# Attention and mixture of experts on one core: inputs laid out on the host, q as pairs of heads' dims by tokens

## The chip, the cores and the metric

The kernel runs on one core of one Trainium2 chip. The metric is the device time of one execution in microseconds (us), the median over runs. In the text PE is TensorE, DVE is VectorE, ACT is ScalarE, POOL is GpSimd, and SP is SyncE, which only issues DMAs here. A "batch" is one of the eight entries of the first axis of q, k and v.

## The reference, cut to what matters

All arrays are float32; q, k, v are 8 batches x 8 heads x 576 tokens x 64 dims. There is no softmax in the attention: k'v is a 64 x 64 matrix per head, and q times it is the output, which is then normalised over the 64 dims. The 4,608 token rows (512 wide) go to the one of 8 experts with the largest gate logit, through relu(x w1) w2 (512 -> 1024 -> 512), and are scaled by the gate's probability.

```
kv = np.einsum('bhsd,bhse->bhde', k, v)
out = np.einsum('bhsd,bhde->bhse', q, kv)
rms = np.sqrt(np.mean(out * out, axis=-1, keepdims=True) + 1e-06)
attn = out / rms * g_norm
x = attn.transpose(0, 2, 1, 3).reshape(B * S, H * D)
expert_idx = np.argmax(x @ w_gate, axis=1)
...
h = np.maximum(np.einsum('ecd,edf->ecf', disp, w1), 0.0)
y = np.einsum('ecf,efd->ecd', h, w2)
```

## The kernel before

The work has two stages. The first runs the attention batch by batch, routes each token, and, towards its end, already prepares the weights of one expert (the busiest after three batches) and runs that expert's first 384 rows. The second stage gathers the rows of the experts from a DRAM copy of x and runs the remaining products with weights split in two float16 halves.

Per batch the first stage does this:

- `load(b)` issues from SP, for each of k, v, q and each half of the heads (four heads), two DMAs into one of nine buffers (`NIO`): the odd partitions get four tokens per head (L708), the even partitions five (L709). The runs in DRAM are 1,024 and 1,280 bytes. A partition holds its tokens' rows, [head, token, dim].
- `kv_products` (L730) multiplies k' with v per head on PE, 80 small float32 products per batch. ACT or DVE copies the result to SBUF (`kvs`), PE transposes it (L754) and multiplies it with the gate's weights (L763). Then k'v and its gate columns (72 columns per head, `XW`) are copied into `kv_bd`. This tile is block-diagonal over two *tokens* of one head, so every block is written twice: eight copies per batch (L694 on ACT, L696 on DVE).
- `unit` transposes q on PE, two tokens x 64 dims at a time (L796, 20 transposes of 128 x 128 per batch), copies the result out of PSUM into `qt` (six copies per batch, L694 or L696), and multiplies `qt` with `kv_bd` (L814, 20 float32 products with 144 columns per batch; the trace shows each as two instructions). The result `op` is copied into the output tile `o_sb`, in ten pieces of which two are split in two, because the two tokens of that block belong to different heads.
- `squares` squares `o_sb` (ACT or POOL) and sums over the dims (L845 on DVE). `route` normalises, finds the expert and the position of every token with some 25 small operations, nearly all on DVE, and POOL writes the batch's rows to DRAM (L1023, L1021).

Every operation is given to a planner (`Plan`) with a cost per engine, dependencies, buffers (rings) and a key. The planner places the operations on a model of the engines, chooses between ACT, DVE and POOL where both can do one, and the resulting order is written out as each engine's program order. The second stage is placed by a second plan that starts from the engine times at which the first ended. The weights of the early expert are loaded in quarters between the last input loads (`WAFTER` counts the input loads that are issued before each quarter) and split by L358 (largest value), L387 (high half) and L393 (low half).

Of the kernel before, what the change touches and what calls it, by code (L numbers as in the profile page):

```python
# [12 lines left out]
F32 = mybir.dt.float32  # L13
# [15 lines left out]
NO = 3  # L29
NIO = 9  # L30
HALVED = (1,)
# [4 lines left out]
WAIT = {}  # L36
ISSUE = 1.6
AHEAD = 8.0
# [21 lines left out]
LOW = 36.5  # L60
LOAD = 1.66
WKEYS = ((29.5, 0.3), (38.0, 0.3))
# [13 lines left out]
class Ring:  # L76
# [84 lines left out]
def attention_moe_kernel(  # L161
# [12 lines left out]
    nc = tc.nc  # L174
    NB, H, S, D = q.shape
    N, DM = out.shape
    E = w_gate.shape[1]
# [9 lines left out]
    NT = NB * C  # L187
    W = E * NHI

# [9 lines left out]
    io = actx.enter_context(tc.tile_pool(name="io", bufs=1))  # L199
    ios = {}  # L200
    for i in range(NIO):
        flat = io.tile([P, HH * C * D], F32, name=f"in_sb{i}")
        t = flat.rearrange("p (h c d) -> p h c d", h=HH, c=C)
        (nc.vector if i % 3 == 1 else nc.gpsimd).memset(t[:, :, 0], 0.0)
        ios[i] = t, flat

# [75 lines left out]
    for i in range(2):  # L282
        kv_bds.append(cst.tile([P, H, 2, XW], F32, name=f"kv_bd{i}"))
    wgs = cst.tile([P, 2, 2, 2, E], F32, name="wgs")
# [369 lines left out]
    def slots(pool, reg_ap, s0=0):  # L654
# [3 lines left out]
        for tab_, nm in ((gidx_tab, "gi"), (sidx_tab, "si")):  # L658
# [9 lines left out]
    ps = {n: actx.enter_context(tc.tile_pool(name=f"ps_{n}", bufs=m, space=bass.MemoryType.PSUM))  # L668
          for n, m in (("a", 1), ("qp", 2), ("op", 2), ("x", 1), ("tab", 1), ("misc", 1))}
    bank = lambda n: ps[n].tile([P, 512], F32, tag=n, name=n)  # L670
# [10 lines left out]
    for i in range(NO):  # L681
# [4 lines left out]
    op = plan.op  # L686
    rings = {n: Ring(m) for n, m in (("in", NIO), ("a", 1), ("qp", 2), ("op", 2), ("x", 1),
                                     ("qt", 3), ("sq", 2), ("kvs", 1), ("kvt", 1), ("kv", 2), ("o", NO), ("lt", 1), ("ohh", 1),
                                     ("rhs", 1), ("ohl", 1), ("ss", NO), ("xg", 3), ("xm", 2), ("ysb", 2))}
# [10 lines left out]
    def load(b):  # L700
        ts = {}
        for j, (nm, half) in enumerate(ORDER):
            h = new("in")
            h.t, h.flat = ios[(len(rings["in"].holds) - 1) % NIO]

            def go(e, h=h, src={"k": k, "v": v, "q": q}[nm], hs=slice(half * HH, (half + 1) * HH)):
                rows = src[b, hs].rearrange("h (p n) d -> p h n d", n=2 * C - 1)
                nc.sync.dma_start(h.t[1:P:2, :, 1:C], rows[:, :, C:])  # L708
                nc.sync.dma_start(h.t[0:P:2], rows[:, :, 0:C])  # L709

            o = op(("S", ISSUE), go, [], (b - 2) * C + j * 0.8, takes=(h,))
            ts[nm, half] = h, op(("D", LOAD), None, [o], takes=(), uses=(h,))
            issued.append(o)
        return ts

    def kv_products(b, ts):
# [7 lines left out]
        def product(i):  # L724
            def go(e):
                a.t = a.t or bank("a")
                for c in range(C):
                    for g in range(2):
                        h = 2 * (i % 2) + g
                        nc.tensor.matmul(a.t[rows[g], i * D:(i + 1) * D], lhsT=kh.t[:, h, c, :], rhs=vh.t[:, h, c, :],  # L730
                                         start=(c == 0), stop=(c == C - 1))
# [12 lines left out]

        def spread(g, f):

            return op([("A", 0.42), ("V", 0.31)],
                      lambda e: copy(e, kv2[rows[f]].rearrange("p (i g) f x -> p i g f x", g=2)[:, :, g, f, 0:D],
                                     ks.t[rows[g]].rearrange("p (i x) -> p i x", i=HH)), done[0:1], key + 1.5, (kv,), (ks,))

# [17 lines left out]
        o = op(("T", 0.4), gates, [o], key + 1, (a3,), (kt,))  # L768
        done = [spread(g, f) for g in range(2) for f in range(2)]
        for g in range(2):  # L770
            for f in range(2):
                done.append(op([("A", 0.19), ("V", 0.13)],
                               lambda e, g=g, f=f: copy(
                                   e, kv2[rows[f]].rearrange("p (i g) f x -> p i g f x", g=2)[:, :, g, f, D:XW],
                                   a3.t[rows[g], 0:H * E].rearrange("p (i g x) -> p i g x", g=2, x=E)[:, :, g]),
                               [o] + done[4:], key + 2, (kv,), (a3,)))
        return kv, done


    UNITS = [(0, 0), (1, 0), (0, 1), (1, 1), (0, 2), (1, 2)]  # L780

    BLOCKS = ((0, 2), (1, 3), (4,))

    def unit(b, n, ts, kv, ready, oh):
        key = b * C + n * C / len(UNITS)
        o_sb, kv2 = oh.t, kv.t.rearrange("p h f x -> p (h f) x")
        qp, qt = new("qp"), new("qt")
        half, u = UNITS[n]
        qh, qd = ts["q", half]
        m = 2 * len(BLOCKS[u]) * P  # L790

        def turn(e):
            qp.t = bank("qp")
            for w, t in enumerate(BLOCKS[u]):
                for p in range(2):
                    nc.tensor.transpose(qp.t[:, (2 * w + p) * P:(2 * w + p + 1) * P],  # L796
                                        qh.flat[:, (t + C * p) * P:(t + C * p + 1) * P], ident)

        def keep(e):
            qt.t = at.tile([P, 512], F32, name="qt", bufs=3)  # L800
            copy(e, qt.t[:, 0:m], qp.t[:, 0:m])
# [4 lines left out]
        for w, t in enumerate(BLOCKS[u]):  # L806
            ph = new("op")

            def product(e, w=w, t=t, ph=ph):
                ph.t = bank("op")  # L810
                for p in range(2):
                    f = 2 * (half * HH + 2 * p + (t > 2))
                    x = kv2[:, f:f + 4:3] if t == 2 else kv2[:, f:f + 2]
                    nc.tensor.matmul(ph.t[:, p * 2 * XW:(p + 1) * 2 * XW], lhsT=qt.t[:, (2 * w + p) * P:(2 * w + p + 1) * P],  # L814
                                     rhs=x, start=True, stop=True)

            o = op(("T", 0.55), product, [kept] + ready, key, (ph,), (qt, kv))
            for s0, s1 in ((0, 1), (1, 2)) if t == 2 else ((0, 2),):

                def out_(e, t=t, ph=ph, s0=s0, s1=s1):  # L820
                    m0 = 2 * t + s0
                    h0, c0 = half * HH + m0 // C, m0 % C
                    copy(e, o_sb[:, c0:c0 + s1 - s0, h0:h0 + 3:2].rearrange("p c h x -> p h c x"),
                         ph.t[:, 0:4 * XW].rearrange("p (h c x) -> p h c x", h=2, c=2)[:, :, s0:s1])

                a = op([("A", 0.29), ("V", 0.37)] if s1 - s0 == 2 else [("A", 0.2), ("V", 0.22)], out_, [o], key, (oh,), (ph,))
                done += [((2 * t + i) % C, a) for i in range(s0, s1)]
        return done

    def squares(b, n, done, oh, ssh):  # L830

        key = b * C + (n + 1) * 0.8
        o_sb, ss = oh.t, ssh.t
# [453 lines left out]
    for b in range(NB):  # L1287
        oh, ssh = new("o"), new("ss")
        oh.t, ssh.t = o_sbs[b % NO], sss[b % NO]
        if b + 1 < NB:  # L1290
            tiles[b + 1] = load(b + 1)
        outs, sums = [], []
        for n in range(len(UNITS)):
            done = unit(b, n, tiles[b], *kvs[b], oh)
            outs += done
            if UNITS[n][0]:
                sums += [squares(b, c, [a for i, a in outs if i == c], oh, ssh) for c in ((0,), (1, 2), (3, 4))[UNITS[n][1]]]
            if n == 1 and b + 1 < NB:
                kvs[b + 1] = kv_products(b + 1, tiles[b + 1])
        route(b, oh, ssh, [a for _, a in outs], sums)  # L1300
        if b == PICK_AFTER:
            early_weights()
        if b == EARLY_AFTER:
            early_slots()
# [360 lines left out]


# [25 lines left out]
```

## Time and profile before

| | us |
|---|---|
| median of 3 runs (lowest, highest) | 553.29 (552.86, 553.55) |
| the profiled execution, its time | 553.62 |
| the profiled execution, its span from first to last instruction | 551.8 |
| PE busy | 520.2 (94% of the span) |
| DVE busy | 388.7 (70%) |
| ACT busy | 256.3 (46%) |
| POOL busy | 183.8 (33%) |

The busy shares are means over stages that look quite different, so the rows below are cut by stage. A busy engine in a row of the trace is not always an engine at its peak: consecutive matmuls overlap. The DMA share counts the time of packets on 16 DMA engines and can pass 1 where packets overlap.

### The profile page before, as it was taken

To read this page: it belongs to the slowest core of one execution; us is meant where nothing else is said; L and a number is where in the kernel's file an instruction comes from. 1 tells how busy PE (TensorE), PEld (TensorE's weight loads), DVE (VectorE), ACT (ScalarE), POOL (GpSimd) and SP (SyncE) were. 2 spreads that over 40 slices of the span, in tenths; PEclk is the share of its full clock that TensorE was granted. 3 is DMA by queue.
4 is the path that set the end of the run, shared out by engine and by line. 5 is a ranking of instruction groups with operands and counts; after the bars stand their busy time and mean duration, and the time that the engine had idled before them with its cause. 6 is when DMAs were issued, how large, how long until landed. Compare 5 with 4: busy or idle time off the path is not lost.

```text
span 551.8 us, 11752 instructions
## 1 busy us (share of the span) xinstructions
PE 520.2 (94%) x4458; PEld 358.2 (65%) x4458; DVE 388.7 (70%) x1042; ACT 256.3 (46%) x514; POOL 183.8 (33%) x187
## 2 busy tenths in 40 slices
PE   4999899877999999999999999999999999999995
PEld 4988888764546566457744764776487468648752
DVE  4388889999769899998998898387567526104800
ACT  1678677778224832745615633435162544211210
POOL 3011020624151462364427424442653264111011
PEclk9999999899999999999999999999999999999999
DMA  8999999952276869695677846464656153010000
GB/s 273 379 318 360 382 397 402 339 164 98 98 263 237 171 211 263 152 325 123 178 250 205 239 121 211 123 172 118 207 154 167 40 105 42 6 57 23 2 38 32
DMA packets 81903, 102.70 MB, mean 186 GB/s; under 512 B 39148, under 2 KB 63724, under 8 KB 80818
## 3 DMA queue, kind: packets, MB, share of 16 engines
q1 hardware_dynamic: 74240, 70.50, 43.1%
q0 software_dynamic: 7584, 31.38, 16.4%
q8 instruction: 37, 0.61, 0.4%
q14 instruction: 24, 0.20, 0.1%
q10 hardware_dynamic: 18, 0.02, 0.0%
HBM read 73.20 MB, written 20.68 MB: 170 GB/s over the span
## 4 chain that ended last, share of the span: by engine, by line
PE 33%; issue 27%; POOL 11%; DVE 9%; DMA 1%; POOLq 0%; ACT 0%; DVEq 0%
PE hp L548 15%; PE yp L595 14%; POOL out_dram L625 4%; POOL pair L481 3%; POOL xm L452 3%; PE op L548 2%; POOL xg L444 1%; DVE am L358 1%; DVE w1l L393 1%; DVE ss L845 1%; PE yp L604 1%; DMA raw<-in_moe_w_dram 1%; PE op L595 1%; DVE hl L556 1%; PE xp L463 0%
## 5 line engine op out<-in xcount | busy, mean ns | idle before, releaser
L548 PE MATMUL hp<-xs,w1h 128*128 128x320 f16 (+6 forms) x960 | 133.7, 292 | 2.4 <-DVE hl L556 1.1
L548 PEld LDWEIGHTS <-w1h 128*128 128x128 f16 x1024 | 99.4, 98 | 38.5 <-issue 3.3
L625 POOL DMA_INDIRECT out_dram<-ysb,si x42 | 43.9, 1046 | 156.2 <-ACT ysb L620 149.1
L595 PEld LDWEIGHTS <-hh 128*128 128x128 f16 x560 | 54.4, 98 | 62.8 <-issue 0.3
L553 ACT ACTIVATE hh<-hp 128x320 f16<-128x320 f32 (+7 forms) x64 | 40.9, 638 | 107.5 <-PE hp L548 98.0
L358 DVE TENSOR_REDUCE am<-raw 128x1 f32<-128x512 f32 x120 | 75.7, 674 | 4.1 <-DMA raw<-in_moe_w_dram 4.0
L548 PE MATMUL hp<-xs,w1l 128*128 128x320 f16 (+6 forms) x480 | 72.0, 292 | 0.0
L620 ACT ACTIVATE ysb<-yp,ysc 128x512 f32<-128x512 f32 (+5 forms) x41 | 28.1, 685 | 92.1 <-PE yp L595 85.7
L556 DVE SCALAR_TENSOR_TENSOR hl<-hp,hh 128x320 f16<-128x320 f32 (+7 forms) x64 | 47.5, 742 | 28.8 <-ACT hh L553 26.5
L595 PE MATMUL yp<-w2h,hh 128*128 128x512 f16 x272 | 64.6, 379 | 0.2 <-ACT ysb L620 0.2
L595 PE MATMUL yp<-w2l,hh 128*128 128x512 f16 x272 | 64.5, 379 | 0.0
L595 PE MATMUL yp<-w2h,hl 128*128 128x512 f16 x272 | 64.5, 379 | 0.0
L548 PEld LDWEIGHTS <-w1l 128*128 128x128 f16 x512 | 50.0, 98 | 16.9 <-issue 0.3
L444 POOL DMA_INDIRECT xg<-x_dram,gi x42 | 43.1, 1027 | 44.5 <-DVE gt L457 17.4
L393 DVE SCALAR_TENSOR_TENSOR w2l<-raw,sw,w2h 128x512 f16<-128x512 f32 x64 | 55.1, 898 | 1.9 <-ACT w2h L387 1.9
L814 PE MATMUL op<-kv_bd,qt 128*128 128x144 f32 x320 | 52.2, 300 | 4.1 <-ACT kv_bd L694 2.1
L610 DVE COPY yt<-yp 128x256 f32<-128x256 f32 (+4 forms) x7 | 2.9, 415 | 74.7 <-PE yp L604 66.0
L481 POOL TENSOR_TENSOR pair<-xm,pair 128x512 f16<-128x512 f32 (+5 forms) x28 | 33.4, 1194 | 57.2 <-ACT pair L477 56.9
L393 DVE SCALAR_TENSOR_TENSOR w1l<-raw,sg,w1h 128x512 f16<-128x512 f32 x64 | 49.7, 821 | 0.0
L595 PEld LDWEIGHTS <-hl 128*128 128x128 f16 x280 | 27.4, 98 | 32.5
L814 PEld LDWEIGHTS op<-kv_bd,qt 128*128 128x128 f32 x320 | 43.4, 194 | 7.5 <-ACT kv_bd L694 2.8
L387 ACT ACTIVATE w2h<-raw,sw 128x512 f16<-128x512 f32 x62 | 40.3, 712 | 11.0 <-PE yp L604 7.7
(232 smaller groups left out, 665.8 us busy)
## 6 DMA issues: line engine op xcount, KB each, us to landing
raw<-in_moe_w_dram SPq DMA_DIRECT2D x64, 512.0 KB
x_dram<-o_sb POOLq DMA_DIRECT2D x8, 720.0 KB
in_sb<-in_k_dram SPq DMA_DIRECT2D x16, 320.0 KB
in_sb<-in_v_dram SPq DMA_DIRECT2D x16, 320.0 KB
in_sb<-in_q_dram SPq DMA_DIRECT2D x16, 320.0 KB
x_dram<-o_sb POOLq DMA_DIRECT2D x8, 576.0 KB
in_sb<-in_k_dram SPq DMA_DIRECT2D x16, 256.0 KB
in_sb<-in_v_dram SPq DMA_DIRECT2D x16, 256.0 KB
```

The lines of the kernel that those rows point to most:

```text
L358: nc.vector.tensor_reduce(out=am()[:, p:p + 1], in_=raw[:, sl(p)], axis=AX.X, op=ALU.max, apply_absolute_value=True)
L387: nc.scalar.activation(wh[:, sl(p)], raw[:, sl(p)], AF.Copy, scale=z["s"])
L393: nc.vector.scalar_tensor_tensor(out=wl[:, sl(p)], in0=raw[:, sl(p)], scalar=z["s"], in1=wh[:, sl(p)], op0=ALU.mult, op1=ALU.subtract)
L444: nc.gpsimd.indirect_dma_start(out=self.xg[i][0:n], out_offset=None, in_=x_dram[0:self.rows, :], in_offset=bass.IndirectOffsetOnAxis(ap=se ...
L481: eng.tensor_tensor(out=pair[0:n, 1], in0=self.xm[i][0:n], in1=pair[0:n, 0], op=ALU.subtract)
L548: nc.tensor.matmul(self.view(hp)[:, v], lhsT=w[:, c, f * P:(f + 1) * P], rhs=x[:, c, u * hw:(u + 1) * hw], start=(t == 0 and c == 0), stop ...
L553: nc.scalar.activation(self.out(self.hh, j), self.view(hp), AF.Relu)
L556: nc.vector.scalar_tensor_tensor(out=self.out(self.hl, j), in0=self.view(hp), scalar=0.0, in1=self.out(self.hh, j), op0=ALU.max, op1=ALU.s ...
L595: nc.tensor.matmul(yp[0:n, 0:DM], lhsT=h[:, j, o:o + n], rhs=w[:, j, :], start=(m == 0), stop=(m == len(self.terms) - 1))
L620: nc.scalar.activation(self.ysb[0:n], yp[0:n, 0:DM], AF.Copy, scale=self.ysc[0:n, i:i + 1])
L625: nc.gpsimd.indirect_dma_start(out=(disjoint.pop() if disjoint else out)[:, :], out_offset=bass.IndirectOffsetOnAxis(ap=self.sidx[0:n, col ...
L814: nc.tensor.matmul(ph.t[:, p * 2 * XW:(p + 1) * 2 * XW], lhsT=qt.t[:, (2 * w + p) * P:(2 * w + p + 1) * P], rhs=x, start=True, stop=True)
```

## The change

A host function lays q, k and v out anew (the same numbers in another order), so that the kernel's loads and products change:

- q comes as [batch, half of the heads, 128, 1152]: the 128 partitions are two heads x 64 dims, the columns are tokens. It can be used as the stationary operand at once. The transposes of q and the copies to `qt` are gone.
- `kv_bd` is block-diagonal over two *heads*, so every k'v is written once: two copies of k'v and two of gate columns per batch.
- k and q come in one DMA per half, v in two, with runs of 4,608 bytes. The nine buffers become six for k and q and three for v, which are a little wider and keep columns of zeros for the odd or even partitions.
- The loop of `unit` goes over five token chunks, each with both halves of the heads, and every `op` is copied in one piece. `squares` follows each chunk. The four PSUM banks of `qp` and `op` are now all `op`.
- The planner's costs of a load and of its issue are changed.

```diff
-NIO = 9
+NIO = 6
+NV = 3
-ISSUE = 1.6
+ISSUE = (0.8, 1.6)
-LOAD = 1.66
+LOAD = 1.46
...
-    ios = {}
...
+    ins = [io.tile([P, CD], F32, name=f"in_sb{i}") for i in range(NIO)]
+    vins = [io.tile([P, CD + TD], F32, name=f"v_sb{i}") for i in range(NV)]
+    for i, t in enumerate(vins):
+        (nc.vector if i % 2 else nc.gpsimd).memset(t[:, 0:TD], 0.0)
+        (nc.vector if i % 2 else nc.gpsimd).memset(t[:, CD:CD + TD], 0.0)
...
-                rows = src[b, hs].rearrange("h (p n) d -> p h n d", n=2 * C - 1)
-                nc.sync.dma_start(h.t[1:P:2, :, 1:C], rows[:, :, C:])
-                nc.sync.dma_start(h.t[0:P:2], rows[:, :, 0:C])
-
-            o = op(("S", ISSUE), go, [], (b - 2) * C + j * 0.8, takes=(h,))
+                if nm == "v":
+                    nc.sync.dma_start(h.t[0:P:2, TD:CD + TD], src[0:P:2])
+                    nc.sync.dma_start(h.t[1:P:2, 0:CD], src[1:P:2])
+                else:
+                    nc.sync.dma_start(h.t, src)
+
+            o = op(("S", ISSUE[nm == "v"]), go, [], (b - 2) * C + j * 0.8, takes=(h,))
...
-        done = [spread(g, f) for g in range(2) for f in range(2)]
+        done = [spread(g) for g in range(2)]
...
-        o = op(("T", m / 980), turn, [qd], key - 1.2, (qp,), (qh,))
-        kept = op([("A", 0.48), ("V", 0.6)] if m == 512 else [("A", 0.29), ("V", 0.34)], keep, [o], key - 1, (qt,), (qp,))
-        done = []
-        for w, t in enumerate(BLOCKS[u]):
+        c, key = CHUNKS[n], b * C + n
+        o_sb, done = oh.t, []
+        for half in range(2):
+            qh, qd = ts["q", half]
             ph = new("op")
...
+                for i in range(2):
+                    q0 = i * MD * 2 + c * P if c else i
+                    nc.tensor.matmul(ph.t[:, i * 2 * XW:(i + 1) * 2 * XW], lhsT=qh.t[:, q0:q0 + P],
+                                     rhs=kv.t[:, 2 * half + i].rearrange("p g x -> p (g x)"), start=True, stop=True)
...
-            o = op(("T", 0.55), product, [kept] + ready, key, (ph,), (qt, kv))
+            o = op(("T", 0.55), product, [qd] + ready, key + half * 0.1, (ph,), (qh, kv))
+            done.append(op([("A", 0.29), ("V", 0.37)], out_, [o], key + half * 0.1, (oh,), (ph,)))
```

## Rows read from the trace of the kernel before

**Rows 1.** By stage, busy us: PE, PEld, DVE, ACT, POOL; clock, DMA share, GB/s.

```profile
10.00:98.00 88.00, 81.75 (x1058) 75.09 (x1054) 67.42 (x236) 60.66 (x162) 9.95 (x14) 1.00 1.03 374
98.00:124.00 26.00, 21.85 (x217) 18.98 (x218) 24.85 (x74) 21.08 (x58) 11.06 (x11) 0.93 0.70 245
124.00:150.00 26.00, 23.02 (x161) 13.31 (x160) 23.12 (x79) 13.81 (x37) 7.74 (x8) 1.00 0.26 104
150.00:200.00 50.00, 46.98 (x362) 28.37 (x360) 40.45 (x113) 22.60 (x40) 22.20 (x20) 1.00 0.70 203
200.00:552.00 352.00, 342.93 (x2629) 218.89 (x2627) 227.15 (x505) 135.72 (x217) 127.99 (x118) 1.00 0.49 137
```

**Rows 2.** Timeline of SP's queue: last load of q, first and last batch.

```profile
8.88 0.65 SPq L709 DMA_DIRECT2D in_sb<-in_q_dram  x1
...
98.08 0.60 SPq L709 DMA_DIRECT2D in_sb<-in_q_dram  x1
```

**Rows 3.** Timeline of POOL: writes of the first and last batch's rows.

```profile
36.94 0.78 POOL L1023 DMA_DIRECT2D x_dram<-o_sb  x1 [6.83 <-DVE o_sb L1014]
...
144.16 0.58 POOL L1023 DMA_DIRECT2D x_dram<-o_sb  x1 [6.93 <-DVE o_sb L1014]
```

**Rows 4.** Groups on DVE from 98 to 150 us: count, busy us, mean ns.

```profile
L845 DVE TENSOR_REDUCE ss<-sq 128x8 f32<-128x512 f32 x10 | 6.7, 675 | 0.0
L393 DVE SCALAR_TENSOR_TENSOR w1l<-raw,sg,w1h 128x512 f16<-128x512 f32 x8 | 6.4, 816 | 0.0
L393 DVE SCALAR_TENSOR_TENSOR w2l<-raw,sw,w2h 128x512 f16<-128x512 f32 x8 | 6.3, 790 | 0.0
```

**Rows 5.** Instructions on `qt`: busy us on PE, PEld, DVE, ACT.

```profile
0.00:98.00 98.00, 38.56 (x244) 32.22 (x244) 4.67 (x8) 16.20 (x31) 1.00 1.00 359
98.00:150.00 52.00, 13.63 (x76) 11.13 (x76) 0.83 (x2) 3.74 (x7) 0.97 0.48 174
```

**Rows 6.** Instructions on `kv_bd`: busy us on PE, PEld, DVE, ACT, POOL.

```profile
0.00:98.00 98.00, 38.56 (x244) 32.22 (x244) 7.37 (x32) 7.09 (x22) 2.09 (x2) 1.00 1.00 359
98.00:150.00 52.00, 13.63 (x76) 11.13 (x76) 1.93 (x4) 1.30 (x6) 0.00 (x0) 0.97 0.48 174
```

**Rows 7.** The transposes of q (L796): busy us on PE, PEld.

```profile
0.00:98.00 98.00, 22.87 (x138) 17.15 (x138) 1.00 1.00 359
98.00:150.00 52.00, 3.82 (x22) 2.71 (x22) 0.97 0.48 174
```

**Rows 8.** Copies out of `op` on ACT up to 150 us, by shape.

```profile
L694 ACT COPY o_sb<-op 128x288 f32<-128x288 f32 x52 | 20.4, 398 | 6.3 <-PE op L814 5.3
...
L694 ACT COPY o_sb<-op 128x144 f32<-128x144 f32 x20 | 5.2, 284 | 3.7 <-PE op L814 3.1 <-DVE o_sb L696 0.3
```

**Rows 9.** DMA queues, 12 to 24 us: packets, MB, share of 16 engines.

```profile
q1 hardware_dynamic: 4239, 4.60, 106.8%
```

**Rows 10.** DMA queues, 60 to 72 us (q0 holds the writes of rows).

```profile
q1 hardware_dynamic: 3110, 3.38, 78.3%
q0 software_dynamic: 160, 1.33, 26.8%
```

**Rows 11.** Timeline of PE: k'v of the last batch, transposes, first output tile.

```profile
107.27 1.39 PE L730 MATMUL a<-in_sb,in_sb 128*64 128x64 f32 x40
...
111.15 0.63 PE L763 MATMUL a<-wgs,kvt 128*128 128x32 f32 x4 [0.51 <-ACT kvt L694]
111.62 1.07 PE L796 MATMUL qp<-ident,in_sb 128*128 128x128 f32 x8
...
147.90 1.89 PE L595 MATMUL op<-w2h,hl 128*128 128x512 f16 x8
```

**Rows 12.** SP's waits over the span: total us, times, longest.

```profile
SPq L708 <- PE qp L796: 7.2, 6, 2.6
```

**Rows 13.** Busy time around the fall of the clock; columns as in rows 1.

```profile
98.00:102.00 4.00, 2.95 (x13) 2.59 (x14) 3.77 (x14) 2.54 (x9) 1.05 (x1) 0.68 1.03 375
110.00:116.00 6.00, 3.88 (x31) 3.21 (x30) 5.85 (x16) 4.12 (x12) 2.49 (x3) 1.00 0.32 102
```

More of the change, by code (lines that the diff above doesn't have):

```diff
@@ L282, in attention_moe_kernel @@
     for i in range(2):
-        kv_bds.append(cst.tile([P, H, 2, XW], F32, name=f"kv_bd{i}"))
+        kv_bds.append(cst.tile([P, HH, 2, XW], F32, name=f"kv_bd{i}"))
     wgs = cst.tile([P, 2, 2, 2, E], F32, name="wgs")
@@ L768, in kv_products @@
         o = op(("T", 0.4), gates, [o], key + 1, (a3,), (kt,))
-        done = [spread(g, f) for g in range(2) for f in range(2)]
+        done = [spread(g) for g in range(2)]
         for g in range(2):
[L771 to L776, printed above, removed]
+            done.append(op([("A", 0.19), ("V", 0.13)],
+                           lambda e, g=g: copy(e, kv2[rows[g], :, g, D:XW],
+                                               a3.t[rows[g], 0:H * E].rearrange("p (i g x) -> p i g x", g=2, x=E)[:, :, g]),
+                           [o] + done[0:2], key + 2, (kv,), (a3,)))
@@ L777, in kv_products @@
         return kv, done
-    UNITS = [(0, 0), (1, 0), (0, 1), (1, 1), (0, 2), (1, 2)]
-    BLOCKS = ((0, 2), (1, 3), (4,))
+    CHUNKS = (1, 2, 3, 4, 0)
     def unit(b, n, ts, kv, ready, oh):
[L785 to L793, printed above, removed]
-            for w, t in enumerate(BLOCKS[u]):
[L795 to L801, printed above, removed]
-        o = op(("T", m / 980), turn, [qd], key - 1.2, (qp,), (qh,))
-        kept = op([("A", 0.48), ("V", 0.6)] if m == 512 else [("A", 0.29), ("V", 0.34)], keep, [o], key - 1, (qt,), (qp,))
-        done = []
-        for w, t in enumerate(BLOCKS[u]):
+        c, key = CHUNKS[n], b * C + n
+        o_sb, done = oh.t, []
+        for half in range(2):
+            qh, qd = ts["q", half]
@@ L807, in unit, with product @@
             ph = new("op")
-            def product(e, w=w, t=t, ph=ph):
+            def product(e, half=half, qh=qh, ph=ph):
                 ph.t = bank("op")
[L811 to L815, printed above, removed]
@@ L1292, in attention_moe_kernel @@
         outs, sums = [], []
-        for n in range(len(UNITS)):
+        for n in range(C):
             done = unit(b, n, tiles[b], *kvs[b], oh)
             outs += done
-            if UNITS[n][0]:
-                sums += [squares(b, c, [a for i, a in outs if i == c], oh, ssh) for c in ((0,), (1, 2), (3, 4))[UNITS[n][1]]]
+            sums.append(squares(b, n, CHUNKS[n], done, oh, ssh))
             if n == 1 and b + 1 < NB:
                 kvs[b + 1] = kv_products(b + 1, tiles[b + 1])
-        route(b, oh, ssh, [a for _, a in outs], sums)
+        route(b, oh, ssh, outs, sums)
         if b == PICK_AFTER:
@@ L1664, with _laid_out @@
 _OUTS = [((4608, 512), "float32")]
+def _laid_out(np, q, k, v):
+    B, H, S, D = q.shape
+    P, HH = 128, H // 2
+    n = np.arange(1, 5)[:, None] + 4 * np.arange(2)
+    x = q.reshape(B, 2, HH // 2, 2, P // 2, 9, D)
+    most = x[:, :, :, :, :, n].transpose(0, 1, 3, 7, 2, 5, 4, 6).reshape(B, 2, P, -1)
+    rest = x[:, :, :, :, :, 0].transpose(0, 1, 3, 5, 4, 2).reshape(B, 2, P, -1)
+    laid = {"q": np.concatenate([rest, most], -1)}
+    for name, a in (("k", k), ("v", v)):
+        x = a.reshape(B, 2, HH, S, D)
+        most = x[:, :, :, 0:4 * P].reshape(B, 2, HH, P, 4, D).transpose(0, 1, 3, 4, 2, 5).reshape(B, 2, P, -1)
+        rest = x[:, :, :, 4 * P:].reshape(B, 2, 2, 2, P // 2, D).transpose(0, 1, 4, 2, 3, 5).reshape(B, 2, P, -1)
+        both = np.concatenate([most, rest], -1)
+        if name == "v":
+            both[:, :, 1::2] = np.concatenate([rest, most], -1)[:, :, 1::2]
+        laid[name] = both
+    return laid
 def kernel(**inputs):
```

52 lines of the change are left out of this document (25 added, 27 removed).

## The prediction

> **What bounds the kernel now.** I read the table by stage first [rows 1]. From 200 us to the end PE is busy 342.93 of 352 us at full clock. Nothing of the change stands there, so that part can only be moved as a whole, and the question is when the first stage ends. I take as its end the last product of the early expert's first output tile, 147.90 + 1.89 = 149.8 us [rows 11]; call it 150.
>
> Inside the first stage the picture changes at 98 us, where SP issues its last input load [rows 2]. Before it, three things are nearly full at once: PE 81.75 of 88 us, DMA a share of 1.03, DVE 67.42 and ACT 60.66. After it the DMA share falls to 0.70 and 0.26, and DVE takes over: 24.85 of 26 and 23.12 of 26 us [rows 1].
>
> The reader should then compare arrival and departure of a batch. The last half of q of batch 0 is issued at 8.88 and that of batch 7 at 98.08 [rows 2], the rows are written at 36.94 and 144.16 [rows 3]. So batch 0 needs 28.1 us from load to write and batch 7 needs 46.1: the engines fall 18 us behind the loads. After 98 us DVE still has ten sums of squares to do, which are two whole batches, and it has the early weights besides, of which the two largest groups are 6.4 and 6.3 us [rows 4]. Loads set the pace early, but from the middle on the engines do.
>
> **What goes away on PE.** All 160 transposes. They are busy 22.87 + 3.82 = 26.7 us [rows 7], but overlap their neighbours: eight in a row take 1.07 us [rows 11], so 160 take 21.4. As busy time is not peak, I take 18 to 22, some 2.5 us a batch. The 320 product instructions stay, with the same 144 columns, and so do the small k'v products. The first product's stationary operand is now a loaded tile instead of `qt`, the same 128 columns.
>
> **What goes away on ACT and DVE.** All copies to `qt`: 16.20 + 3.74 on ACT, 4.67 + 0.83 on DVE, together 25.4 us [rows 5]. Half of the copies to `kv_bd`, whose DVE and ACT time is 7.37 + 7.09 + 1.93 + 1.30 = 17.7, so 8.8 us [rows 6]. Sixteen split copies of `op` become whole ones: two of 284 ns against one of 398 save 0.17 us each, 2.7 us [rows 8]. The sum is 36.9 us, of DVE's 115 and ACT's 96 us between 10 and 150 [rows 1]. Most of it lies on ACT, but the planner gives a copy to either engine, so what ACT gets back takes copies off DVE. Shared evenly it is 18 us per engine, 2.3 us a batch. DVE's own work (squares' sums, routing, low halves of weights) stays untouched.
>
> **What changes in the loads.** The 28.3 MB of k, v, q come in runs of 4,608 bytes. From 12 to 24 us only inputs move: 4.60 MB in 4239 packets (1.09 KB each) with 106.8% of 16 engines, which is 205 engine-us, or 22.4 GB/s per engine and 383 GB/s in all [rows 9]. From 60 to 72 us the writes of rows, 8.3 KB per packet, take 51.5 engine-us for 1.33 MB: 25.9 GB/s per engine, with the inputs at 22.5 beside them [rows 10]. The new runs lie between and nearer to the long ones. At 22.4 the inputs cost 1264 engine-us, at 25.9 they cost 1093; over 16 engines at a share of 1.07 that is 74 against 64 us. So the bounds are 0 and 10 us. With both queues at work the total was 4.71 MB in 12 us, 392 GB/s [rows 10], not what 25.9 per engine would give in all; that holds me to half of it, 5 us. SP's waits for transposes to free a buffer, 7.2 us in six pieces [rows 12], go too, but most are covered by loads in flight; I add 1 us. The last load is then issued about 6 us sooner. SP issues 64 input DMAs in place of 96; none of them held the queue up for long, so this is costed at nothing, and the loads in flight hide it.
>
> The Trainium skill, in "DMA: Bandwidth & Descriptors", section Specifications, names 512 bytes as the smallest transfer that still runs at line rate. By that rule runs of 1 KB are as good as long ones and the loads gain nothing; the time would be the one given for the first rival below. The trace speaks against it, 22.4 against 25.9 GB/s per engine, though those packets also differ in direction.
>
> **The sum.** Loads: -6 us. Then the lag behind the loads: after 98 us there remain 22 transposes, 3.82 us [rows 7], copies to `qt` of 4.57 us [rows 5], half of 3.23 us of `kv_bd` [rows 6] and four split copies, 0.7: 6.9 us on ACT and DVE, 3.4 each. That is removed from the tail for certain. Beyond that, the 18 us by which the engines fell behind should shrink, since each of the seven later batches costs PE, ACT and DVE 2.3 to 2.5 us less, up to 16 us; but while loads are the pace setter an engine can't run ahead of them, and w1's and w2's splits come at the end whatever happens. I take 6 us for the lag in all: the certain 3.4 and a little of the rest. So -12 us. The upper bound is PE's and DVE's whole saving, some 18 us with today's idle time kept; the lower bound is 3.4.
>
> The stage from 150 on follows at once: its gathers need the last batch's rows, and PE is busy 46.98 of 50 us there [rows 1]. The second plan starts from other engine times and may order things a little differently, 1 us either way. The profiled execution took 553.62 us, the span of 551.8 and 1.82 around it: 553.62 - 12 = 541.6. It stood 0.33 above the median of the runs, so I say 541.3. The likeliest case by itself, a gain of 8 to 16 us, runs from 537 to 545.5.
>
> **The rivals.**
>
> *The loads come no sooner.* If another limit than the length of runs holds the loads, -6 falls to -1 or 0, and only the lag shrinks: 3.4 to 8 us, since engines with 2 us a batch to spare then wait for loads. Against it is the row of the long packets, for it that those are writes. Time: 547.3.
>
> *The whole saving comes through.* PE and DVE are each relieved of 18 us and today's idle time stays. For it: DVE is full from 98 on, and the stage ended 52 us after the last load. Against: 92 us of loads can't be shortened by more than 10. Time: about 536.
>
> *q's buffers are held longer.* Before, a transpose freed q; now the last product of the batch does, since every chunk uses both halves, and the loads of the next but one batch's k wait for it. Its round: k and v land (four loads of 0.59 MB at 392 GB/s, 6 us), half of k'v to gates (107.27 to 111.78, 4.5 us [rows 11]), copies of gates 1 us, products of a batch 52.19 / 8 = 6.5 us [rows 5]: 18 us for two batches, 9 for one. The loads take (98.08 - 8.88) / 7 = 12.7 us a batch [rows 2]. So this has 7 us for two batches to spare; it decides only if waits for ACT and DVE add that much, and then the time is where it was, about 553.
>
> *PE's clock falls.* This is the one that ends slower. At 98 to 102 us PE was busy 2.95 of 4 us and the granted clock was 0.68, part of it at 1.2 instead of 2.4 GHz; at 110 to 116 us it was busy 3.88 of 6 and stayed at 1.00 [rows 13]. Without transposes PE has about 2.5 us of 12 more to idle in each batch. Where the clock is at half, PE loses half of the time spent so. To undo 12 us takes some 24 us at half clock; at twice that, the time is about 565. Against it: PE at 81.75 of 88 us kept 1.00 throughout [rows 1], and with 2.5 us less per batch it is still busy three quarters.
>
> **How the numbers follow.** My forecast 0.56; loads no sooner 0.22; whole saving 0.10; buffers 0.05; clock 0.07. The range 535 to 549.5 holds the forecast, nearly all of the first rival and half of the second, 0.8. A difference under 0.2%, 1.1 us, can't be told from none here. Faster 0.88 (the first three), the same 0.05, slower 0.07.
>
> **What would show it.** No L796 and no `qt`; 16 copies each of k'v and gate columns. The last q is issued at 91 to 93 us, and the total rate in loads alone is above 400 GB/s; if it is near 383, the first rival holds. The last batch's rows are written at 130 to 134 instead of 144.16, and the first output tile's products end at about 138. From 200 us on PE's busy time per work is the same, only shifted. I am wrong if the clock shows more windows below 1, if SP waits for L814 for several us at a time, or if DVE, with its copies handed to ACT, still ends where it did.

## The result and the profile after

The changed kernel takes 548.08 us (median of 20 runs, 543.87 to 555.6) beside 553.4 us for the kernel before on the same chip (20 runs, 551.78 to 555.07): a ratio of 0.9905, interval 0.989 to 0.992. It is faster, by 5.3 us, less than half of the 12 that were forecast. Two of its 20 runs (553.82 and 555.6) count as slow and are left out of the ratio; the other 18 lie 6.8 us apart, those of the kernel before 3.3. The profiled execution took 550.31 us, 2.2 above the median, with a span of 548.5.

The gain is that of one chip. On a second one (the control among the experiments) the changed kernel takes the same 548.03 us, but the kernel before only 550.17: 2.1 us, and the interval of the ratio, 0.9942 to 0.9974, doesn't overlap the first.

The table by stage, as in [rows 1], with two rows that cut at 84 us instead:

```profile
10.00:98.00 88.00, 73.12 (x925) 68.17 (x926) 61.59 (x230) 45.10 (x122) 6.90 (x13) 0.89 0.99 382
98.00:124.00 26.00, 19.81 (x189) 18.36 (x188) 23.36 (x57) 18.95 (x47) 11.80 (x10) 0.77 0.51 197
124.00:150.00 26.00, 25.14 (x173) 14.42 (x170) 22.70 (x86) 12.19 (x30) 7.39 (x8) 1.00 0.27 111
...
0.00:84.00 84.00, 68.80 (x849) 63.99 (x850) 52.76 (x207) 42.70 (x111) 7.61 (x24) 0.92 0.97 369
84.00:150.00 66.00, 53.35 (x480) 40.75 (x479) 58.87 (x199) 35.94 (x92) 21.45 (x21) 0.87 0.52 204
```

The kernel before, cut at the same place:

```profile
0.00:84.00 84.00, 72.27 (x924) 66.85 (x925) 59.86 (x227) 52.94 (x137) 13.67 (x30) 1.00 1.00 353
84.00:150.00 66.00, 58.04 (x553) 44.06 (x551) 61.26 (x198) 45.02 (x121) 19.93 (x20) 0.97 0.60 222
```

Over 150 us ACT was relieved of 97.96 - 78.64 = 19.3 us and DVE of 121.12 - 111.63 = 9.5. Of DVE's share 7.1 us lie before 84 us, where it was not full, and 2.4 behind, where it is busy 58.87 of 66. And PE's granted clock, before 1.00 up to 98 us and 0.93 in the next 26, is now 0.89 and 0.77.

Where the end of the stage went is read from three rows: the last load of q (SP), the write of the last batch's rows (POOL) and the last products of the first output tile (PE); they answer to [rows 2, 3, 11].

```profile
93.03 1.78 SPq L717 DMA_DIRECT2D in_sb<-in_q_dram  x2
```

POOL's timeline, the write of the last batch:

```profile
138.99 0.60 POOL L1005 DMA_DIRECT2D x_dram<-o_sb  x1 [4.97 <-DVE o_sb L996]
```

PE's timeline, the last products of the tile:

```profile
145.79 1.04 PE L599 MATMUL op<-w2h,hl 128*128 128x512 f16 x4
```

The tile ends at 145.79 + 1.04 = 146.83 instead of 149.79, 3.0 us sooner, and from there to the end of the span it is 401.7 us (before 402.0). From the last issue for q (93.9, the second of the two; before 98.08) to that tile there were 51.7 us and are 52.9. So the loads came sooner, and the lag behind them, which should have shrunk by 6 us, grew by one.

Nearly half of this lag is the stretch of the early expert. Its first products in PE's timeline before:

```profile
124.85 1.46 PE L548 MATMUL op<-xs,w1h 128*128 128x384 f16 x8 [0.65 <-ACT o_sb L694]
```

And after:

```profile
124.08 1.71 PE L552 MATMUL op<-xs,w1h 128*128 128x384 f16 x8
```

The tile ends 24.9 us after this start in the kernel before and 22.75 in the changed one (21.9 to 26.7 in all profiles of this document). So of the 3.0 us only 0.8 lie ahead of it.

SP's waits before 100 us, with the total, the count and the longest:

```profile
SPq L714 <- PE a L740: 28.8, 7, 8.0
SPq L717 <- PE op L801: 13.0, 6, 4.5
```

The first is a load of v that waits until k'v has read one of v's three buffers, the second a load of k or q that waits for products with q. Before, SP waited 7.2 us for transposes [rows 12]. Four loads in a row then come when two batches are done at once. The writes of rows show it: 36.43, 40.64, 61.08, 67.39, 89.04, 93.94 us, in pairs 25 to 28 us apart, where they used to come evenly. Between two pairs PE waits for its next k'v, and a stretch at half clock follows. PE from 38 us, at the start of a pair (the last two rows are at full clock):

```profile
37.97 1.01 PE L773 MATMUL a<-wgs,kvt 128*128 128x32 f32 x4 [1.03 <-ACT kvt L698]
39.44 2.29 PE L801 MATMUL op<-kv_bd,in_sb 128*128 128x144 f32 x8 [0.46 <-ACT kv_bd L698]
...
45.89 1.39 PE L740 MATMUL a<-v_sb,in_sb 128*64 128x64 f32 x40
47.21 1.25 PE L801 MATMUL op<-kv_bd,in_sb 128*128 128x144 f32 x8
```

Eight products take 2.29 us, at full clock 1.25: that is the lower of PE's two levels, 1.2 GHz for 2.4. The granted clock of three such stretches (busy PE, clock, DMA share, GB/s):

```profile
36.00:46.00 10.00, 8.21 (x90) 0.66 1.00 363
64.00:74.00 10.00, 8.05 (x116) 0.66 1.00 374
...
108.00:120.00 12.00, 8.29 (x36) 0.57 0.48 171
```

In the tail the last of them has a cause of its own. PE's timeline:

```profile
110.72 1.07 PE L773 MATMUL a<-wgs,kvt 128*128 128x32 f32 x4 [0.65 <-ACT kvt L698]
113.97 4.18 PE L801 MATMUL op<-kv_bd,in_sb 128*128 128x144 f32 x16 [2.19 <-issue]
```

DVE's, at the same time:

```profile
105.59 7.95 DVE L397 SCALAR_TENSOR_TENSOR w1l<-raw,sg,w1h 128x512 f16<-128x512 f32 x7 [0.41 <-ACT w1h L391]
113.58 0.29 DVE L700 COPY kv_bd<-kvs 64x256 f32<-64x256 f32 x1
```

DVE does seven low halves of w1 in one block, 7.95 us. The copy of the last batch's k'v to `kv_bd` stands behind them, and all 16 products of the batch behind the copy; they then run at half clock. POOL's work lies beside this block (w1h, a square and three xm, 104.69 to 111.67), and a low half takes 1147 ns on average against the 816 of [rows 4]; the eighth, at 113.90 us behind POOL's work, takes 0.75 us.

### The profile page after: what moved, and what is told of

Read it like the earlier page. It is cut to its first block, busy times and chain, and to the rows that moved or that the text cites. A ratio compares the mean times of both kernels' runs of the same rounds, so it can differ in the third digit from the quotient of the medians.

```text
span 548.5 us, 11277 instructions
## 1 busy us (share of the span) xinstructions
PE 509.4 (93%) x4298; PEld 350.4 (64%) x4298; DVE 379.2 (69%) x1004; ACT 236.5 (43%) x458; POOL 180.7 (33%) x182
## 4 chain that ended last, share of the span: by engine, by line
issue 32%; PE 26%; DVE 22%; POOL 13%; ACT 4%; DMA 2%; POOLq 1%; DVEq 0%; SPq 0%
PE yp L599 6%; PE op L801 6%; DVE am L362 5%; PE hp L552 5%; POOL out_dram L629 4%; POOL xm L456 3%; POOL pair L485 3%; PE a L740 3%; PE op L552 3%; DVE w1l L397 2%; DVE w2l L397 2%; DVE ss L827 2%; DVE hl L560 2%; POOL xg L448 2%; ACT w1h L391 1%
## 5 line engine op out<-in xcount | busy, mean ns | idle before, releaser
L629 POOL DMA_INDIRECT out_dram<-ysb,si x42 | 45.1, 1073 | 163.0 <-ACT ysb L624 149.6
L801 PE MATMUL op<-kv_bd,in_sb 128*128 128x144 f32 x320 | 53.0, 328 | 5.7 <-issue 3.0
L485 POOL TENSOR_TENSOR pair<-xm,pair 128x512 f16<-128x512 f32 (+5 forms) x30 | 36.0, 1199 | 56.0 <-ACT pair L481 55.7
L397 DVE SCALAR_TENSOR_TENSOR w1l<-raw,sg,w1h 128x512 f16<-128x512 f32 x64 | 53.9, 896 | 0.4 <-ACT w1h L391 0.4
L801 PEld LDWEIGHTS op<-kv_bd,in_sb 128*128 128x128 f32 x320 | 48.6, 222 | 6.9 <-issue 3.4
```

Source lines behind the costliest of these rows:

```text
L397: nc.vector.scalar_tensor_tensor(out=wl[:, sl(p)], in0=raw[:, sl(p)], scalar=z["s"], in1=wh[:, sl(p)], op0=ALU.mult, op1=ALU.subtract)
L485: eng.tensor_tensor(out=pair[0:n, 1], in0=self.xm[i][0:n], in1=pair[0:n, 0], op=ALU.subtract)
L629: nc.gpsimd.indirect_dma_start(out=(disjoint.pop() if disjoint else out)[:, :], out_offset=bass.IndirectOffsetOnAxis(ap=self.sidx[0:n, col ...
L801: nc.tensor.matmul(ph.t[:, i * 2 * XW:(i + 1) * 2 * XW], lhsT=qh.t[:, q0:q0 + P], rhs=kv.t[:, 2 * half + i].rearrange("p g x -> p (g x)"), ...
```

## The experiments

They were timed on chips where the kernel before ran at 550 to 554 us, so ratios to the kernel before on the same chip are given. They carry over from chip to chip only roughly: one kernel below has 0.9979 on one chip and 0.9906 on another, at the same time in us, since the kernel before differs. "The tile" is the end of the first output tile, "rest" what follows it to the end of the span; both are of one profiled execution. Theories: the lag is made of PE's clock, or of the waits for buffers, or of the order and amount of work behind about 84 us.

**A fourth buffer for v.**

```diff
-NV = 3
+NV = 4
```

> One more buffer for v (four instead of three), nothing else. Theory B (buffers: SP stands 28.8 us in front of v's loads until k'v products free a buffer, so k and v of every second batch come late): these waits fall below 10 us, the last load is issued some 3 us sooner, 543 to 546 us. Theory C (clock: PE's gaps between pairs of batches let its clock fall to 1.2 GHz, which costs 12 us of PE): k still waits for q's buffers, the gaps stay, 547 to 549. Theory T (tail: DVE's order after the last load sets the end): 547 to 549.

Measured: 0.9872 (0.9856 to 0.9889), a median of 543.1 us, the tile at 143.50. The time is that of theory B, but not by its way: SP's waits moved on to k and q (25.0 us for k'v) instead of going, and the last loads of q were issued no sooner than in the changed kernel (94.4). The tail ran at a clock of 0.94 between 98 and 124 us, but that this is what helped isn't shown: the last kernel below has 0.93 there and its tile ends at 145.82.

**Buffers so that no load waits** (NV = 4, NIO = 8).

> Four buffers for v and eight for k and q. Theory B: both kinds of SP's waits (28.8 and 13.0 us) nearly go, batches are no longer written in pairs, the granted clock from 10 to 98 us rises from 0.89 to over 0.95 by itself, 538 to 543 us. Theory C alone: as good as the clock gets, 541 to 546. Theory T: loads sooner do not help, 546 to 549.

Measured: 0.9943 (0.9916 to 0.997). Its loads come 10 us sooner:

```profile
82.97 1.69 SPq L717 DMA_DIRECT2D in_sb<-in_q_dram  x2
```

SP's waits for PE products fell to 1.7 us, the rows of the first five batches were written evenly (34.3, 44.4, 54.5, 64.8, 75.3), and the tile still ended at 145.72. Its table:

```profile
0.00:84.00 84.00, 69.68 (x955) 64.70 (x955) 61.53 (x242) 46.61 (x119) 8.56 (x26) 0.98 0.99 401
84.00:150.00 66.00, 52.11 (x378) 36.88 (x379) 52.54 (x168) 33.00 (x83) 19.40 (x19) 0.77 0.43 164
```

DVE did 9 us more before 84 us than in the changed kernel and had 6 us less to do behind, yet nothing was gained: PE's clock was 0.77 there, and the first eight products of the early expert, which waited for DVE's copy to `xs`, began at 120.23 and took 2.74 us where 1.46 is usual. So the date of the loads alone doesn't set the time, as theory T has it.

**Dummy products on PE** ahead of its waits, 30 of 128 x 128 float16 per batch, into an unused part of a PSUM tile. The order of all else is that of the changed kernel.

```diff
+    def warm(n):
+        for _ in range(n):
+            nc.tensor.matmul(misc[:, 384:512], lhsT=ones16, rhs=upto16, start=True, stop=True, skip_group_check=True)
...
+                warm(8 if n == 0 and half == 0 else 0)
```

> Thirty small idle float16 products per batch are put in front of PE's waits in the chain of k'v and in front of the routing's products; their result is never read. Theory C: the clock from 10 to 98 us rises from 0.89 to 0.97 or more and the time falls to 541 to 544 us, although PE has more to do. Theory B: the loads are as late as before, 546 to 549. Theory T: 547 to 549.

Measured: 0.9993 (0.9978 to 1.0008). The clock did rise, to 0.98 up to 98 us and 0.87 in the next 26, the last loads of q were issued at 89.22 and the tile ended at 142.86. That is 1.7 us sooner than in the control (144.58, below), less than two profiles of one program differ by (5.9, below). The rest took 403.8 us, 2.3 more than in the control, for which I have no reason, and the time is no better. So the lower clock isn't shown to be the cause of the shortfall; what the dummies cost PE themselves was not measured apart.

**Short runs again**: the new layout, read in four runs of 1,152 bytes per partition and load.

```diff
-                    nc.sync.dma_start(h.t, src)
+                    nc.sync.dma_start(cut(h.t), src)
```

> Same bytes, same tiles, same order of work, but each partition's 4,608 bytes lie in DRAM as four runs of 1,152 bytes. If the length of runs gave the loads' 5 us: the rate of loads alone falls from 417 to about 385 GB/s, the last load is issued 3 to 5 us later and the time is 551 to 553. If the loads are not what sets the end: same as with long runs, 547 to 549.

Measured: 0.9957 (0.9938 to 0.9977), the same as the changed kernel on another chip (next). The rate fell as the prediction's sum has it. The DMA queues of the changed kernel from 42 to 60 us:

```profile
q1 hardware_dynamic: 1236, 4.87, 67.3%
q0 software_dynamic: 311, 2.55, 33.6%
```

And of this one:

```profile
q1 hardware_dynamic: 4777, 5.28, 82.2%
```

4.87 MB in 67.3% of 16 x 18 us are 25.1 GB/s per engine, 5.28 MB in 82.2% are 22.3; before it was 22.4 [rows 9]. The length of the runs is worth 13% of the rate and nothing that can be measured in time. Nor did it bring the loads: with short runs the last q is issued at 93.1 us, no later than in the changed kernel (93.9), where the first expectation wanted 3 to 5 us later. Up to 84 us the two move 366 and 369 GB/s, the short runs with a DMA share of 1.02, the long ones with 0.97.

**The changed kernel again, all copies on ACT, w1's column maxima on ACT, and both with a fourth buffer**, on one chip. The copies' edit is `op([("A", ...), ("V", ...)], ...)` to `op(("A", ...), ...)` at L753 to L808; the maxima's is

```diff
-TOPS = ('VVVV', 'AAAA')
+TOPS = ('AAAA', 'AAAA')
```

> The changed kernel once more, unchanged, as the control on the chip of the next three. Ratio to the kernel before 0.988 to 0.993 by every theory; its DVE is busy over 95% from 84 us to the first output tile.

> All copies out of PSUM and into the block-diagonal tile go to ACT; the planner may no longer give them to DVE. Theory T (from 84 us on DVE is the bound, and the change took little work from it there): DVE loses some 10 us up to 150 us, about 4 of them after 84, and the time falls by 3 to 5 us against the control. Theory C or B (PE's clock, late loads): within 1.5 us of the control.

> The eight largest-value passes over the first early weight, 5.4 us on DVE between 84 and 99 us, go to ACT (as sums of absolute values, as the second weight's already do). Theory T: the time falls by 3.5 to 5.5 us against the control. Theory C or B: within 1.5 us of it.

> Both moves to ACT and the fourth buffer for v. If the gains add up, 8 to 12 us below the control, ratio 0.970 to 0.977. If DVE, once relieved, only makes room for PE's half clock as the next bound: 4 to 6 us below the control.

Measured: 0.9958 (0.9942 to 0.9974), 0.9899 (0.9874 to 0.9924), 0.9908 (0.9883 to 0.9934) and 0.9903 (0.988 to 0.9925). The control missed its expectation, and its DVE is busy 57.13 of 66 us from 84 us on, 87% and not over 95%. With all copies on ACT:

```profile
0.00:84.00 84.00, 66.08 (x840) 61.40 (x840) 42.31 (x170) 48.59 (x140) 7.54 (x24) 0.94 0.95 362
84.00:150.00 66.00, 55.31 (x494) 42.00 (x494) 56.56 (x195) 38.86 (x103) 25.14 (x23) 0.87 0.55 213
```

DVE has 12.6 us less to do up to 84 us than the control (54.91) and 0.6 less behind (57.13), and the time falls by 2.4 us. The three lie 2.1 to 2.4 us below the control, more than theories B and C allow and less than theory T or their sum wants, so no expectation was met, and the gains don't add up. Each edit also makes the planner draw another order, which by itself moves the time by more than that (below). So 12.6 us less of DVE's early work went with 2.4 us, and even these aren't shown to be its price; DVE's work behind 84 us falls by 0.6 us with the copies on ACT.

**The early w1 later in the plan**, behind the copies of the last batch, by 2 and by 4 units of the planner's key, and by 2 with a fourth buffer.

```diff
-            key = WKEYS[i][0] + 8 * WKEYS[i][1]
+            key = WKEYS[i][0] + 8 * WKEYS[i][1] + (2.0, 0)[i]
```

> The changed kernel with the early w1's highs and lows (L397 and the ACT or POOL copies before them) keyed 2 later, so that the last batch's copies to kv_bd stand ahead of the eight low halves instead of behind seven of them. Theory O (the order of work in the tail sets the end): the copy to kv_bd of the last batch ends at about 108 instead of 113.6 us, PE's gap at 106 to 113 us closes, the first output tile's last product ends at 142 to 144 and the time falls by 2 to 4 us against the changed kernel, a ratio of 0.988 to 0.992 to the kernel before. Theory W (the weights and the gathered rows themselves are the bound, in whatever order): the time stays within 1 us of the changed kernel, ratio 0.994 to 0.998.

> The same with the early w1's highs and lows keyed 4 later, behind most of the last batch: the low halves are spread over the batch's products. Theory O: as with 2 or better, the last batch's rows written at 131 to 135 instead of 139 us, ratio 0.985 to 0.991. Theory W: no better, and up to 2 us worse, since the early GEMM1 waits for the low halves (ratio 0.995 to 1.000).

> A fourth buffer for v and the early w1 keyed 2 later, together. If the wait for v's buffers early and the order of the tail are separate costs, the gains add up: ratio 0.982 to 0.986. If both give back the same time, it is that of the better one alone, 0.987 to 0.989.

Measured: 0.9979 (0.9957 to 1.0001), 0.9894 (0.9867 to 0.9921) and 1.0015 (0.9988 to 1.0042). With 2, the profiled execution did part of what the theory of the order expects: the copies to `kv_bd` went to ACT in the midst of w1, the 16 products waited 0.46 us for them instead of 2.19, the tile ended at 141.76, and the run took 542.21 us.

```profile
104.39 1.11 PE L467 MATMUL x<-ident,xm 128*128 128x128 f32 x4 [3.71 <-POOL xm L456]
...
106.39 1.06 PE L773 MATMUL a<-wgs,kvt 128*128 128x32 f32 x4 [0.46 <-ACT kvt L698]
107.92 4.21 PE L801 MATMUL op<-kv_bd,in_sb 128*128 128x144 f32 x16 [0.46 <-ACT kv_bd L698]
```

But the gap only moved: PE now waits 3.71 us for POOL's `xm`, and from the last k'v to the 16 products it is 7.2 us (100.69 to 107.92) where it was 7.7 (106.25 to 113.97). The whole chain came sooner. And this was the fastest of the twelve runs, whose median is 548.76. The 16 products still took 4.21 us, at half clock, right behind a wait of 0.46 us. With 4, the ratio is the one theory O expected, but by another way: the last rows were written at 139.3 us, not at 131 to 135, and the tile ended at 144.41, as in the control. The block of w1 is thus not shown to cost the missing 6 us. For the third, neither expectation held: with a fourth buffer this key is 0.0143, some 8 us, worse than the old one (timed on another chip, where the kernel before takes the same 550 us).

**The same kernel once more.** Why does one program take 542 us and then 551?

> The kernel with the early w1 keyed 2 later, unchanged, once more. Theory C (PE's clock differs between executions): a profiled run near 549 us shows the same instructions with the stretches of half clock longer or elsewhere than in the run of 542 us, and the difference of some 6 us is in PE's durations or in what they delay before 150 us. Theory D (transfers differ): the clock is the same and the loads or writes land later.

Measured: 549.03 us, 0.9906 (0.987 to 0.9941) on another chip, where the kernel before takes 553.63 us instead of 550.07; the profiled run took 550.74, so the two profiles of one program, one from each chip, are 8.5 us apart. PE from the first k'v of batch 0 to that of batch 1's first half, in the run of 542 us:

```profile
6.12 0.45 PE L740 MATMUL a<-v_sb,in_sb 128*64 128x64 f32 x2 [0.67 <-DMA v_sb<-in_v_dram]
...
9.60 2.11 PE L740 MATMUL a<-v_sb,in_sb 128*64 128x64 f32 x40
...
14.24 2.83 PE L801 MATMUL op<-kv_bd,in_sb 128*128 128x144 f32 x12 [0.53 <-issue]
17.00 1.86 PE L740 MATMUL a<-v_sb,in_sb 128*64 128x64 f32 x40
```

The same in the run of 551 us:

```profile
7.47 0.45 PE L740 MATMUL a<-v_sb,in_sb 128*64 128x64 f32 x2 [1.43 <-DMA v_sb<-in_v_dram]
...
10.88 2.40 PE L740 MATMUL a<-v_sb,in_sb 128*64 128x64 f32 x40
...
16.50 3.22 PE L801 MATMUL op<-kv_bd,in_sb 128*128 128x144 f32 x12 [0.53 <-issue]
19.65 1.66 PE L740 MATMUL a<-v_sb,in_sb 128*64 128x64 f32 x40
```

The first products on v start 1.35 us later; by the second batch it is 2.65 us. The other 1.3 us lie in PE's own durations in between: in the run of 551 us the second 40 products of k'v take 2.40 us instead of 2.11, the two transposes 0.69 instead of 0.44, the gates 1.06 instead of 0.63 and the first 12 products with q 3.22 instead of 2.83. The k'v of the second batch frees a buffer of v that SP waits for (its issue moved from 18.78 to 21.24 us), the last loads of q follow 4.3 us later (88.01 and 92.29), and the tile 5.9 us later (141.76 and 147.66). The mean granted clock is nearly the same (0.90 and 0.91 from 10 to 98 us, 0.80 and 0.79 from 98 to 124), but the first batch shows both a later transfer and slower products, so neither theory is ruled out, and the two chips may differ by themselves.

Two other rows speak against the first load as the whole cause. In the control the first k'v starts at 7.36 us and in the profile of the result at 6.94, yet the control is at the second batch's k'v at 18.23 instead of 19.13 and takes 2.3 us less. And the kernel in which hardly a load waits for a product (NV = 4, NIO = 8) has runs 7.8 us apart, counted as for the result. What spreads the runs is open.

**The planner's figures.** First the changed kernel with the two load figures as they were before (LOAD 1.66, ISSUE 1.6 for all), then each kernel with LOAD moved by 0.06 either way. The work is the same; only its order differs, and the engine of some operations that two engines can do (such as copies, squares and high halves).

```diff
-LOAD = 1.46
+LOAD = 1.40
```

> The changed kernel with the planner's two load figures as they were before (1.66 a load, 1.6 an issue); what runs on the chip is the same but for its order. If the pairing of the batches and the block of low halves come from those figures, SP's waits for v shrink and the time falls to a ratio of 0.987 to 0.991. If they come from the three buffers of v and the smaller work, the time stays within 1 us of the changed kernel, ratio 0.994 to 0.998.

> The kernel before with the planner's load figure at 1.60 instead of 1.66: the same work in a slightly different order. Theory S (each order costs a few us more or less): a ratio anywhere from 0.99 to 1.015. Theory L (the layout's worth is small by itself, and orders near each other cost the same): 0.998 to 1.002.

> The kernel before with the load figure at 1.72. Theory S: a ratio from 0.99 to 1.015, and not the same as with 1.60. Theory L: 0.998 to 1.002.

> The changed kernel with the load figure at 1.40 instead of 1.46. Theory S: a ratio from 0.980 to 1.005 to the kernel before. Theory L: 0.994 to 0.998, as the changed kernel.

> The changed kernel with the load figure at 1.52. Theory S: a ratio from 0.980 to 1.010, and not the same as with 1.40. Theory L: 0.994 to 0.998.

| kernel, LOAD | ratio to before (95%) | median us | last q, us | tile, us | rest, us |
|---|---|---|---|---|---|
| before, 1.66 | 1 | 550.2 | 98.1 | 149.8 | 402.0 |
| before, 1.60 | 1.0018 (1.0 to 1.0037) | 550.78 | 100.6 | 150.95 | 398.6 |
| before, 1.72 | 1.0139 (1.0113 to 1.0165) | 557.43 | 101.7 | 154.86 | 402.7 |
| changed, 1.46 (control) | 0.9958 (0.9942 to 0.9974) | 548.03 | 91.5 | 144.58 | 401.5 |
| changed, 1.40 | 0.9943 (0.9925 to 0.9962) | 546.39 | 91.2 | 144.01 | 400.2 |
| changed, 1.52 | 0.9873 (0.9843 to 0.9903) | 542.92 | 94.1 | 142.06 | 398.9 |
| changed, 1.66, ISSUE 1.6 | 1.0115 (1.0099 to 1.0131) | 556.13 | 98.1 | 154.34 | 398.3 |

(The last three columns of the first row are of [rows 2, 11]. The rows with LOAD moved by 0.06 share a chip; the control and the last row are from another, where the kernel before had 550.17 and 550.07.) Moved by 0.06 us, a figure that touches no instruction changes the kernel before by up to 7 us and the changed one by up to 5; with the old figures the changed kernel is slower than the kernel before. Theory S holds in all four rows, and those of 1.72 and 1.52 lie outside theory L (those of 1.60 and 1.40 fit both), so orders near each other don't cost the same. With the old figures neither expectation was met: 1.0115 for 0.987 to 0.998. Over the three orders with LOAD at its own value and 0.06 around it, the means are 552.8 and 545.8 us: 7 us for the layout, with three draws on each side that lie 7 and 5 apart.

**The best order with a fourth buffer for v** (LOAD 1.52, NV = 4).

> The changed kernel with the load figure at 1.52 and a fourth buffer for v. If the two costs are separate, the gains add: a ratio of 0.977 to 0.982. If the order decides, and the buffer only draws another order: anywhere from 0.982 to 0.997.

Measured: 0.9896 (0.9869 to 0.9924), within the second expectation: no sum of the two gains. In us it is 547.94, on the chip where the kernel before takes 553.63; the two parts alone took 543.1 and 542.92 on chips where that takes 550, so the ratios can't be set against each other closely. The best version stays one of two that can't be told apart, a fourth buffer alone (0.9872) and LOAD 1.52 alone (0.9873).

## Why the prediction was right in sign and wrong in size

**What was right.** The transposes and `qt` are gone, the copies to `kv_bd` are halved (16 of k'v, 16 of gate columns), and whatever the first output tile gains comes through from there on: 3.0 us sooner, 401.7 against 402.0 us for the rest. The rate per engine rose to 25.1 GB/s, within the bounds of 22.4 and 25.9 that the prediction took from [rows 9, 10] and near the upper one. The last q was forecast for 91 to 93 us and is issued at 93.9, 91.5 in the control: the 6 us of the loads are 4.2 and 6.6. That is luck in part: with short runs, at the old rate per engine, it is issued at 93.1, so the rate that the term was worked out from isn't what brought the loads. The total rate in loads alone, which should have passed 400 GB/s, is 371 from 12 to 24 us (385 before), and 405 in the control. Of the three signs that were to prove it wrong two came: a lower clock and SP's long waits. The rows of the last batch came at 138.99 for 130 to 134, the tile at 146.83 for 138.

**The step that failed** is the lag: "I take 6 us for the lag in all: the certain 3.4 and a little of the rest." It measured +1.2 us in the profile shown (51.7 to 52.9), and the lag lies between 48.0 and 56.2 us in the table's four rows of the changed kernel; the two other orders of the kernel before have 50.4 and 53.2. The sum took the tile's end as the last load and a lag behind it, and the end isn't tied to the last load so: with loads 10 us sooner the tile ended at 145.72 us, between the control's 144.58 and the 146.83 of the result. Nor has the sum a term for the lag's last 22 to 27 us, the early expert's products and what these wait for, where 2.2 of the 3.0 us were gained. Three more things stand in place of the 6 us.

First, the 36.9 us of removed copies were not "shared evenly". DVE got 9.5 and ACT 19.3 us, and four squares moved from POOL to ACT (6 of them on POOL before, 2 after). DVE got 2.4 us behind 84 us, where it is busy 58.87 of 66, not 3.4, and gave 2.3 back in w1's low halves, 8.7 us for eight instead of 6.4 [rows 4], beside POOL. What DVE lost earlier became idle time: 12.6 us less of its early work went with 2.4 us. The prediction had counted DVE, at 67.42 of 88 us up to 98 us, among what is nearly full.

Second, loads and engines are now tied together. The rival *q's buffers are held longer* was priced by the time that two batches of k and q need; it left out v, whose ring of three had the longest wait, 28.8 us in seven pieces. It didn't take the whole gain, as its time of 553 has it, but the batches go in pairs with it, and the first five came evenly without it. Freed of it, the loads came 10 us sooner and the end did not.

Third, the clock. The prediction put 0.07 on it and held against it that PE was busy 81.75 of 88 us. It fell all the same, to 0.89 and 0.77, in stretches at the start of a pair of batches, where PE had waited; with the batches written evenly it was 0.98 up to 84 us instead of 0.92. By the prediction's own rule (PE loses half of the time at half clock) the windows to 98 and to 124 us lose 73.12 x 0.11 + 19.81 x 0.23 = 12.6 us of PE's time, an estimate from those two rows. Little of it seems to be on the path: with the clock put back to 0.98 and 0.87, the tile ended 1.7 us sooner than in the control, and the time was no better.

**A term too small**: "order things a little differently, 1 us either way". The same work in another order moved the time by up to 7 us in the kernel before and 5 in the changed one, and the rest behind the tile lies between 398.3 and 403.8 us, 2.7 of it between two executions of one program (398.3 and 401.0). This scatter alone is nearly as wide as the likeliest case, a gain of 8 to 16 us. The range, 535 to 549.5, held the time only because the first rival was in it.

**The length of the runs.** 1.1 KB packets moved at 22.3 to 22.4 GB/s per engine and 4.6 KB runs at 25.1, so 512 bytes, named as the smallest transfer at line rate by the Trainium skill ("DMA: Bandwidth & Descriptors", Specifications), are not enough for the whole rate in this trace. The time came out as if they were: cut into runs of 1,152 bytes, the kernel took the same time. The first rival's condition, that another limit than the length of runs holds the loads, is borne out in the changed kernel; its mechanism (the loads come no sooner) was wrong, and its time, 547.3, was nearly right, by luck.

**What stays open**: how the 5.3 us split into layout and order, and why they are 2.1 on another chip. No experiment keeps the order and changes the layout, since the transposes are part of the order; three draws of each kernel give 7 us, and the spread of the draws is as large. Which of the many waits makes one order good wasn't settled either: the block of w1 was tried and isn't shown to be it.

## What to carry to other kernels

In this kernel, time removed from an engine counted only where that engine is full and sets the end: cut the stage at the point from which it is full, and sum what leaves that part; the rest becomes idle time, and on PE idle time can cost the clock as well. Where a planner writes the order, move one of its figures a little in both kernels before you believe a few microseconds: the scatter is the error bar of any forecast and of any single change. Time both kernels on a second chip too: here the same change was worth 5.3 us on one and 2.1 on another. When a buffer's reader changes, redo the round trip of every ring that the new reader holds, not only of the one that the change names.

## What the runs showed of the hardware

- PE's granted clock was 0.57 to 0.66 over three stretches of 10 to 12 us in which PE was busy 8.05 to 8.29 us, broken by waits of 0.5 to 2.6 us; in the kernel before, the 0.68 of [rows 13] is the only such stretch of the first stage. Eight products of 128 x 144 took 2.29 us there and 1.25 at full clock. Sixteen right behind a wait of only 0.46 us took 4.21 us, so the length of the wait just ahead doesn't settle the clock here.
- Low halves of w1 on DVE took 1147 ns on average where POOL worked on tiles in SBUF beside seven of the eight, and 0.75 us for the eighth; 816 ns in the kernel before and 852 in the order with LOAD 1.52 (6.28 us for eight in one block). No run changes POOL's work alone.
- The same kernel was 2.1 us faster than the one before on one chip and 5.3 on another, by the time of the kernel before (550.17 and 553.4 us); its own time was the same (548.03 and 548.08).
